# A transformer block's last product by Strassen's seven block products, 256 tokens at a time

## The chip, the cores and the metric

The kernel runs on one core of a Trainium2 chip, in one launch. Its engines are TensorE (PE; PEld is its weight load), VectorE (DVE), ScalarE (ACT), GpSimd (POOL) and SyncE (SP). SP issues all the DMAs here. The metric is the time of one execution in microseconds (us) on the device. A measurement of this kernel can tell a difference of about 0.3%.

## The reference, cut to what matters

Three layers follow each other: chunked attention, a SoLU layer with a layer norm, and a hard-swish layer. The change is in the hard-swish layer, the last one:

```python
def _moe2_ref(x, w_in, w_out):            # x: 3072 x 512, w_in: 512 x 2048, w_out: 2048 x 512
    h = x @ w_in
    relu6 = np.clip(h + 3.0, 0.0, 6.0)
    g = h * relu6 / 6.0
    return (g @ w_out).astype(np.float32)
```

The first product below is `x @ w_in`, the second is `g @ w_out`. The weights arrive as float64 words; the output is float32.

## The kernel before

To come close to float32 accuracy with operands of type float32r, each operand of a product is split into a high part (a copy into the type float32r, by ACT) and a low part (what remains, by DVE). The helper is `split`, lines 221 to 223. A product then takes three matmuls: high by high, high by low and low by high.

**Attention and SoLU stage** (to about 450 us). A step of the loop at line 707 does one tile of 128 tokens: both products of the SoLU layer and the attention of later tiles. Beside it the weights of the hard-swish layer are converted from float64 words (ACT, POOL, DVE) and stored to DRAM as float32 (`w2_store`, line 316). At the end of the last step come `split_x2(0)` and `split_w2(0)`, and behind them `ln_t` of the last tile and the twelve pieces of the last group's second SoLU product (`m2`).

**Hard-swish stage** (from about 450 us to the end). The tokens are taken in 8 groups of 384, the 2048 hidden columns in 16 blocks `f` of 128; a step is one pair (group, f), 128 steps in all.
- `g3` (line 619) makes one hidden block for the 384 tokens: 4 parts of the 512 inputs by 3 matmuls, so 12 matmuls with 384 moving columns. ACT takes the relu out of PSUM (line 628), DVE the min and product (line 629), and `split` makes the two parts `gh` and `gl`.
- `g4` (line 635), two steps later, adds this block's share to the output: for each of three tiles of 128 tokens, three matmuls with 512 moving columns, 9 in all. The three accumulators are scaled and stored at the end of a group (lines 649 to 654).

Each step's weights, high and low, are split in the first group and then stay in SBUF for all eight groups.

The program is in a fixed order: each engine runs its own instructions in the order in which the functions are called, and waits on semaphores where it needs another engine. SP is in order too, so a DMA that waits holds up the DMAs behind it.

## Time and profile before

| what | before |
|---|---|
| median of 3 runs | 989.15 us (988.51 to 990.86) |
| the profiled execution, span | 988.3 us |
| PE busy | 97% |
| DVE, ACT, POOL busy | 53%, 41%, 16% |
| chain that ended last | PE 89%, DVE 5%, DMA 3% |
| DMA | 86.72 MB, 88 GB/s over the span |

The times come from unprofiled runs, the rows from one profiled execution, whose span lies 0.85 us under the median. Matmuls are pipelined: a row's duration is the time that one takes from start to end, longer than the distance from one start to the next. How fast PE goes is read from the starts.

### The profile page before, as it was taken

What the parts mean: (1) busy time and instruction counts of PE and PEld (TensorE: products, weight loads), DVE (VectorE), ACT (ScalarE), POOL (GpSimd) and SP (SyncE); (2) the same over time, 40 slices, a digit from 0 to 9 for tenths busy, and PEclk for the clock granted to TensorE, in tenths of its full rate; (3) what the DMA queues carried; (4) which work ended last, traced back from release to release, by engine and by line L of the source; (5) the groups of instructions that cost most, each with busy time, mean ns of one, the idle gap of its engine ahead of it and who ended that gap; (6) DMA issues with size and microseconds to landing.
All of it is one profiled execution on the core that took longest, in us unless ns stands there. A gap on an engine that the chain in (4) does not pass through costs nothing.

```text
span 988.3 us, 15688 instructions
## 1 busy us (share of the span) xinstructions
PE 963.0 (97%) x6160; PEld 847.7 (86%) x6160; DVE 518.9 (53%) x921; ACT 408.5 (41%) x716; POOL 156.9 (16%) x123
## 2 busy tenths in 40 slices
PE   5899899999999999999999999999999999999998
PEld 4677788888888888899999999999999999999997
DVE  6999978787878776465532232232322322323222
ACT  2567635555564554344533232232332322323322
POOL 3637732423324240000000000000000000000000
PEclk9799999999999999999999999999999999999999
DMA  9897247656856672233401010010010010100000
GB/s 184 166 218 171 68 144 192 157 160 176 180 157 160 191 167 79 91 104 124 159 1 65 0 57 8 1 64 1 1 64 1 22 43 1 65 1 1 33 1 33
DMA packets 131769, 86.72 MB, mean 88 GB/s; under 512 B 105072, under 2 KB 117360, under 8 KB 131696
## 3 DMA queue, kind: packets, MB, share of 16 engines
q1 hardware_dynamic: 131696, 85.72, 33.4%
q8 instruction: 49, 0.80, 0.3%
q14 instruction: 24, 0.20, 0.1%
HBM read 64.72 MB, written 20.97 MB: 87 GB/s over the span
## 4 chain that ended last, share of the span: by engine, by line
PE 89%; DVE 5%; DMA 3%; issue 1%; SPq 1%; ACT 0%; POOL 0%; DVEq 0%; POOLq 0%
PE ph L625 27%; PE acc L646 27%; PE m L569 13%; PE h L484 11%; PE tp L453 2%; PE sc L397 2%; PE tp L541 2%; PE tp L371 2%; PE tp L372 1%; DMA km<-in_k_dram 1%; PE tp L384 1%; PE tp L435 1%; DMA mk<-in_mem_k_dram 1%; DMA w1raw<-in_moe_w_in_dram 0%; DMA w2d<-w2t 0%
## 5 line engine op out<-in xcount | busy, mean ns | idle before, releaser
L646 PE MATMUL acc<-w,gh 128*128 128x512 f32 x768 | 238.8, 392 | 0.0
L629 DVE SCALAR_TENSOR_TENSOR r<-r,ph 128x384 f32<-128x384 f32 x128 | 70.9, 554 | 278.3 <-ACT r L628 278.3
L628 ACT ACTIVATE r<-ph,three 128x384 f32<-128x384 f32 x128 | 74.4, 582 | 284.9 <-PE ph L625 284.9
L646 PEld LDWEIGHTS acc<-w,gh 128*128 128x128 f32 x768 | 142.3, 188 | 22.7
L646 PE MATMUL acc<-w,gl 128*128 128x512 f32 x384 | 151.1, 394 | 0.0
L625 PE MATMUL ph<-x,w 128*128 128x384 f32 x768 | 144.5, 336 | 0.0
L625 PE MATMUL ph<-x2h,w 128*128 128x384 f32 x512 | 141.0, 337 | 0.0
L625 PEld LDWEIGHTS ph<-x,w 128*128 128x128 f32 x768 | 136.0, 188 | 5.4
L223 DVE TENSOR_TENSOR gl<-r,gh 128x384 fp32r<-128x384 f32 x128 | 71.5, 559 | 75.7 <-ACT gh L222 75.7
L222 ACT ACTIVATE gh<-r 128x384 fp32r<-128x384 f32 x128 | 67.2, 525 | 80.1 <-DVE r L629 80.1
L625 PEld LDWEIGHTS ph<-x2h,w 128*128 128x128 f32 x512 | 93.7, 188 | 2.5
L569 PE MATMUL m<-lnh,wol 128*128 128x384 f32 x256 | 88.6, 346 | 0.9 <-POOL wol L313 0.9
L569 PE MATMUL m<-lnh,woh 128*128 128x384 f32 x256 | 88.4, 345 | 0.8 <-ACT woh L195 0.5
L569 PE MATMUL m<-lnl,woh 128*128 128x384 f32 x256 | 88.6, 346 | 0.3 <-DVE lnl L238 0.3
L625 PE MATMUL ph<-x2l,w 128*128 128x384 f32 x256 | 86.1, 336 | 0.0
L646 PEld LDWEIGHTS acc<-w,gl 128*128 128x128 f32 x384 | 72.0, 188 | 16.0
L484 PE MATMUL h<-w1h,xh 128*128 128x512 f32 x168 | 70.8, 421 | 0.0
L208 POOL TENSOR_SCALAR w2t<-w2t 128x512 f32<-128x512 f32 x32 | 64.9, 2040 | 28.2 <-ACT w2t L201 28.2
L484 PE MATMUL h<-w1h,xl 128*128 128x512 f32 x168 | 67.1, 400 | 1.7 <-DVE xl L238 1.7
L484 PE MATMUL h<-w1l,xh 128*128 128x512 f32 x168 | 66.6, 396 | 0.0
L234 ACT ACTIVATE lnh<-tp 128x512 fp32r<-128x512 f32 x41 | 24.3, 598 | 70.6 <-PE tp L541 70.5
L625 PEld LDWEIGHTS ph<-x2l,w 128*128 128x128 f32 x256 | 48.0, 188 | 2.5
(134 smaller groups left out, 1343.6 us busy)
## 6 DMA issues: line engine op xcount, KB each, us to landing
v<-in_v_dram SPq DMA_DIRECT2D x176, 56.0 KB
w2raw<-in_moe_w_in_dram SPq DMA_DIRECT2D x16, 512.0 KB
w2raw<-in_moe_w_out_dram SPq DMA_DIRECT2D x16, 512.0 KB
w2d<-w2t SPq DMA_DIRECT2D x32, 256.0 KB
...
```

What stands on the lines that cost most here:

```text
L208: ENG[eng].tensor_scalar(out=tf, in0=tf, scalar1=U_LO, scalar2=U_HI, op0=ALU.max, op1=ALU.min)
L222: ACT.activation(out=hi, in_=r, func=AF.Copy)
L223: (eng or DVE).tensor_tensor(lo, r, hi.bitcast(F32), ALU.subtract)
L234: ACT.activation(out=hi, in_=r, func=AF.Copy)
L371: PE.transpose(pt[:, j, 0:P], kn[i % 2][:, h:h + 2].rearrange("t h d -> t (h d)"), ident)
L397: PE.matmul(sc[64 * x:64 * x + 64, c, s], qb[:, p, c].rearrange("k y t -> k (y t)"), kT[:, p, c], start=True, stop=True)
L484: PE.matmul(h[:, f], a[:, kt], w[kt][:, f * 512:(f + 1) * 512], start=n == 0, stop=n == 3 * NKT - 1)
L569: PE.matmul(acc, w[fc // 2][:, fc % 2, dc * P:(dc + 1) * P], a[:, fc], start=n == 0, stop=n == len(todo) - 1)
L625: PE.matmul(ph, w[:, dc * P:(dc + 1) * P], xg[gi][a][:, dc], start=j == 0, stop=j == len(todo) - 1)
L628: ACT.activation(out=r, in_=ph, func=AF.Relu, bias=three, scale=1.0)
L629: DVE.scalar_tensor_tensor(out=r, in0=r, scalar=6.0, in1=ph, op0=ALU.min, op1=ALU.mult)
L646: PE.matmul(acc_t[t], a[:, sl], w, start=f == 0 and n == 0, stop=f == NF2 - 1 and n == 2)
```

## The change

A step now takes two hidden blocks (256 hidden columns) for a group of 256 tokens: 12 groups of 8 steps, 96 steps. `g3` makes both hidden blocks in one PSUM tile: 24 matmuls of 256 columns. The 2 x 2 blocks of `g` (two hidden blocks, two tiles of tokens) and the 2 x 2 blocks of the weights (two hidden blocks, two halves of the output columns) are multiplied by Strassen's method: seven products of sums and differences of blocks in place of eight, each with three matmuls of 256 columns, 21 in all. POOL makes the sums of `g` blocks (`act3`), ACT and DVE split them (`split3`), and the seven products are accumulated over a group in four PSUM banks and combined at its end by ACT, POOL and DVE (`g_out`, `g_end`).

The sums of weight blocks are made by POOL in the SoLU stage (`sum_pair`, stored to DRAM), read back and split (`prep`). A step's weights for the second product are 7 blocks of 128 x 256, high and low. They don't all fit: the steps 1, 4 and 7 of a group share one place in SBUF, so their split blocks are kept in DRAM and loaded again each time (`load_b`, seven DMAs). The attention and SoLU code keeps its order; some of its tiles get other places.

The diff, cut:

```diff
-    x2d = [dp.tile([P, NKT, G1], F32, name=f"x2d{i}") for i in range(NG)]
-    w2d = [dp.tile([P, 2, 512], F32, name=f"w2d{i}") for i in range(NF2)]
+    x2d = dp.tile([P, NKT, NT], F32, name="x2d")
+    w2d = [[dp.tile([P, 2, 512], F32, name=f"w2d{i}_{j}") for j in range(NF2 // 2)] for i in range(2)]
...
-        SP.dma_start(out=w2d[f][:, part], in_=raw["w2t", u].bitcast(F32))
+        SP.dma_start(out=w2d[part][f // 2][:, f % 2], in_=raw["w2t", u].bitcast(F32))
...
+    TG = 2 * P
+    NB = NT // TG
+    NS = NF2 // 2
+    USERS = (1, 4, 7)
+    B5_HOME = ("lh0", "lh1", "wb0", "wb1", "lh1", "ll1", "ll0", "lh1")
...
+    def load_pair(j):
+        raw["pair"] = T("xal", [P, 2, 2, 256], name="pair")
+        SP.dma_start(out=raw["pair"], in_=w2d[1][j].rearrange("p f (h c) -> p f h c", h=2))
+
+    def sum_pair(j):
+        w, t = raw["pair"], T("x2r", [P, 5, 256], name="sums")
+        POOL.tensor_tensor(t[:, 0:2], w[:, :, 0], w[:, :, 1], ALU.add)
+        POOL.tensor_tensor(t[:, 2], w[:, 0, 0], w[:, 1, 1], ALU.add)
+        POOL.tensor_tensor(t[:, 3], w[:, 0, 1], w[:, 1, 1], ALU.subtract)
+        POOL.tensor_tensor(t[:, 4], w[:, 1, 0], w[:, 0, 0], ALU.subtract)
+        SP.dma_start(out=b5f[j], in_=t)
...
+        for sl, t in parts:
+            split(t, b5[j][:, sl, 0], b5[j][:, sl, 1])
+        for k in range(2):
+            split(d[:, k], b2[j][k][:, 0], b2[j][k][:, 1])
...
+    def load_b(j):
+        for u in (2, 3, 4, 1, 0):
+            SP.dma_start(out=b5[j][:, u].bitcast(F32), in_=b5_d[j][:, u])
+        for n in (1, 0):
+            SP.dma_start(out=b2[j][n].bitcast(F32), in_=b2_d[j][:, n])
...
+    def g3(gi, j):
+        n = gi * NS + j
+        ph = pp.tile([P, 2, TG], F32, tag=("tp0", "tp1", "tp2", "sc")[n % 4], name="ph")
+        for k in range(2):
+            w = w2i[2 * j + k]
+            todo = [(dc, wl, xl) for dc in range(NKT) for wl, xl in ((0, 0), (0, 1), (1, 0))]
+            for m, (dc, wl, xl) in enumerate(todo):
+                PE.matmul(ph[:, k], w[:, wl, dc * P:(dc + 1) * P], xg[gi][xl][dc],
...
+    def act3(gi, j):
+        n = gi * NS + j
+        ph = ph_t.pop(n)
+        rt = home(("pn", "pe")[n % 2], 896, F32)
+        r = rt[:, 0:512]
         ACT.activation(out=r, in_=ph, func=AF.Relu, bias=three, scale=1.0)
         DVE.scalar_tensor_tensor(out=r, in0=r, scalar=6.0, in1=ph, op0=ALU.min, op1=ALU.mult)
-        gh = T(("kn0", "kn1", "q0")[n % 3], [P, 512], F32R, name="gh")[:, 0:G1]
-        gl = T(("km0", "km1", "q1")[n % 3], [P, 512], F32R, name="gl")[:, 0:G1]
-        split(r, gh, gl)
-        g_t[gi, f] = (gh, gl)
-
...
-    def g4(gi, f):
-                    acc_t[t] = late[0].tile([P, DM], F32, tag=f"m{t}", name="acc")
-                else:
-                    acc_t[t] = pp.tile([P, 2, DM], F32, tag="h", name="acc")[:, 0]
-            sl = slice(t * P, (t + 1) * P)
-            for n, (a, w) in enumerate(((gh, wh), (gh, wl), (gl, wh))):
-                PE.matmul(acc_t[t], a[:, sl], w, start=f == 0 and n == 0, stop=f == NF2 - 1 and n == 2)
-        if f == NF2 - 1:
-            for t in range(GT):
...
+    def split3(gi, j):
+        n = gi * NS + j
+        q = home(("pn", "pe")[n % 2], 896, F32).rearrange("p (b t) -> p b t", t=P)
+        s = home("xh", 512, F32).rearrange("p (b t) -> p b t", t=P)
+        tags = (("xah", "xal"), ("lh0", "ll0"))[n % 2]
+        ga = gA[n] = [extra(t)[:, 0:384].rearrange("p (b t) -> p b t", t=P) for t in tags]
+        split(q[:, 0:7:3], *ga)
+        tags = (("lh1", "ll1"), ("wb0", "wb1"))[n % 2]
+        gs = gS[n] = [extra(t).rearrange("p (b t) -> p b t", t=P) for t in tags]
+        split(s, *gs)
...
+    PRODUCTS = ((1, "A", 2, 5, 2), (3, "A", 0, 5, 3), (4, "A", 1, 5, 4), (5, "S", 0, 2, 1), (2, "S", 1, 2, 0),
+                (7, "S", 3, 5, 1), (6, "S", 2, 5, 0))
+    PLACE = {1: (0, 0), 3: (0, 1), 4: (1, 0), 5: (2, 0), 2: (2, 1), 7: (3, 0), 6: (3, 1)}
...
+    def g4(gi, j):
+        n = gi * NS + j
+        ga, gs = gA.pop(n), gS.pop(n)
+        for p, which, blk, wide, u in PRODUCTS:
+            a = ga if which == "A" else gs
+            w = b5[j][:, u] if wide == 5 else b2[j][u]
+            out = M(p)
+            for m, (al, wl) in enumerate(((0, 0), (0, 1), (1, 0))):
+                PE.matmul(out, a[al][:, blk], w[:, wl],
+                          start=j == 0 and m == 0 and PLACE[p][1] == 0, stop=j == NS - 1 and m == 2, skip_group_check=True)
...
+    def g_out(gi):
+        e = home("xl", 512, F32).rearrange("p (n c) -> p n c", n=2)
+        e1, e3, e4 = T("e5", [P, 1, 256], name="e1")[:, 0], e[:, 0], e[:, 1]
+        o1, o2 = T("xo0", [P, 512], name="o"), T("xo1", [P, 512], name="o")
+        o_t[:] = o1, o2, e3, e4
+        for t, n in ((e1, 1), (e3, 3), (e4, 4)):
+            ACT.activation(out=t, in_=M(n), func=AF.Copy, scale=1.0 / 6.0)
+        POOL.tensor_tensor(o1[:, 0:256], e1, e4, ALU.add)
+        POOL.tensor_tensor(o2[:, 256:512], e1, e3, ALU.add)
+
+    def g_end(gi):
+        o1, o2, e3, e4 = o_t
+        c11, c12, c21, c22 = o1[:, 0:256], o1[:, 256:512], o2[:, 0:256], o2[:, 256:512]
+        for o, n, sign, t in ((c12, 5, 1, e3), (c21, 2, 1, e4), (c11, 5, -1, c11), (c22, 2, -1, c22),
+                              (c11, 7, 1, c11), (c22, 6, 1, c22)):
+            DVE.scalar_tensor_tensor(out=o, in0=M(n), scalar=sign / 6.0, in1=t, op0=ALU.mult, op1=ALU.add)
+        for t, o in enumerate((o1, o2)):
+            SP.dma_start(out=out[gi * TG + t * P:gi * TG + (t + 1) * P, :], in_=o)
 
...
+            if m % 2:
+                if m < NTILE - 1:
+                    load_pair(m // 2 - 3)
+            elif m > STEADY:
+                sum_pair(m // 2 - 4)
+            if m == NTILE - 2:
                 load_x2(0)
-                load_w2f(0)
-                load_w2f(1)
+                load_prep()
+                load_prep()
             if m == NTILE - 1:
-                split_x2(0)
-                split_w2(0)
-                load_w2f(2)
+                split_x2(0, 0)
+                split_x2(0, 1)
+                load_wi(0)
+                prep()
+                prep()
+                split_wi(0)
+                load_wi(1)
         for j in range(4):
...
+            if j in (1, 6):
+                prep()
+            if j in (2, 5, 8):
+                w = (j + 1) // 3
+                split_wi(w)
+                load_wi(w + 1)
...
+        LAG = 2
+        for n in range(len(steps) + LAG):
             if n < len(steps):
-                gi, f = steps[n]
...
+                gi, j = steps[n]
+                g3(gi, j)
+                act3(gi, j)
+                if n + 4 < NS:
+                    split_wi(n + 4)
+                    if n + 6 < NS:
+                        load_wi(n + 6)
+                if n in (1, 2, 4, 7):
...
+                    store_prep()
+                if gi + 1 < NB:
+                    if j == 3:
                         load_x2(gi + 1)
-                    if f == 14:
-                        split_x2(gi + 1)
-            if n >= 2:
-                g4(*steps[n - 2])
+                    if j in (5, 6):
+                        split_x2(gi + 1, j - 5)
+            if n >= LAG:
+                gi, j = steps[n - LAG]
+                g4(gi, j)
+                if j in USERS and (gi > 0 or j == USERS[-1]):
+                    k = (USERS.index(j) + 1) % 3
+                    if not (gi == NB - 1 and k == 0):
+                        load_b(USERS[k])
+                if j == NS - 1:
+                    g_out(gi)
+            if n < len(steps):
+                split3(*steps[n])
+            if n >= LAG and j == NS - 1:
+                g_end(gi)
 
```

`USERS` are the steps that share a place; in `PRODUCTS` a row is the product's number, which set of `g` blocks it takes, the block in it, the width of the weight tile and the block there. `M(n)` is the accumulator of product n: products 1 and 3 share a bank, 5 and 2, 7 and 6; product 4 has one alone.

On PE, near the end of the program, one `g3` and the first two thirds of one `g4` stood like this (`ph` is the hidden block, `acc` an accumulator per tile of tokens, `gh` and `gl` the parts of `g`):

```order
L625 MATMUL ph_8863<-x2_8373,w2_5378 128x384 x12
L646 MATMUL acc_8503<-w2_5306,gh_8821 128x512 [waits Activation_49]
L646 MATMUL acc_8503<-w2_5307,gh_8821 128x512
L646 MATMUL acc_8503<-w2_5306,gl_8822 128x512 [waits DVE_49]
L646 MATMUL acc_8507<-w2_5306,gh_8821 128x512
L646 MATMUL acc_8507<-w2_5307,gh_8821 128x512
```

Now `g4` of a group's first step stands behind 24 matmuls of `g3`; here are the last matmul of `g3` and then the products 1, 3 and 4 (`acc_5272`, a tile of two banks), 5 and the beginning of 2 (`acc_5273`); `b_xah`, `b_xal`, `b_lh1`, `b_ll1` hold the parts of the `g` blocks and sums:

```order
L732 MATMUL ph_10087<-b_xah_4844,b_wa6_5022 128x256
L784 MATMUL acc_5272<-b_lh0_4959,b_xah_4844 128x256 [waits Activation_49]
L784 MATMUL acc_5272<-b_lh0_4959,b_xah_4844 128x256
L784 MATMUL acc_5272<-b_lh0_4959,b_xal_4845 128x256 [waits DVE_49]
L784 MATMUL acc_5272<-b_lh0_4959,b_xah_4844 128x256 x2
L784 MATMUL acc_5272<-b_lh0_4959,b_xal_4845 128x256
L784 MATMUL acc_5272<-b_lh0_4959,b_xah_4844 128x256 x2
L784 MATMUL acc_5272<-b_lh0_4959,b_xal_4845 128x256
L784 MATMUL acc_5273<-b_kn1_4961,b_lh1_5156 128x256 [waits DVE_49]
L784 MATMUL acc_5273<-b_kn1_4961,b_lh1_5156 128x256
L784 MATMUL acc_5273<-b_kn1_4961,b_ll1_5157 128x256
L784 MATMUL acc_5273<-b_kn0_4960,b_lh1_5156 128x256 x2
```

Nine matmuls of 512 columns became 21 of 256, and at a group's start product 1 waits for ACT and products 5 and 7 for DVE, which read these banks for the last group's result.

On SP, between two groups stood three stores of the output and one load of tokens:

```order
L654 DMA out_0_dram<-o_7991 128x512 [waits DMAHW7_49,Activation_49]
L654 DMA out_0_dram<-o_7994 128x512 [waits DMAHW0_49,DVE_49]
L654 DMA out_0_dram<-o_7997 128x512 [waits DMAHW1_49,Activation_49]
L605 DMA x2raw_8313<-x2d7_75 128x1536 [waits DMAHW6_49]
L654 DMA out_0_dram<-o_8474 128x512 [waits DMAHW3_49,Activation_49]
```

Now the seven loads of step 1's weights (`b5d1` and `b2d1` in DRAM to `b_lh1`, `b_km1`, `b_km0`) stand ahead of the stores:

```order
L706 DMA b_lh1_5156<-b5d1_94 128x512 [waits DMAHW1_49,PE_49]
L706 DMA b_lh1_5156<-b5d1_94 128x512 [waits DMAHW2_49,PE_49]
L706 DMA b_lh1_5156<-b5d1_94 128x512 [waits DMAHW3_49,PE_49]
L706 DMA b_lh1_5156<-b5d1_94 128x512 [waits DMAHW4_49,PE_49]
L706 DMA b_lh1_5156<-b5d1_94 128x512 [waits DMAHW5_49,PE_49]
L708 DMA b_km1_5202<-b2d1_97 128x512 [waits DMAHW6_49]
L708 DMA b_km0_5201<-b2d1_97 128x512 [waits DMAHW7_49]
L806 DMA out_0_dram<-o_10551 128x512 [waits DVE_49]
L806 DMA out_0_dram<-o_10552 128x512 [waits DMAHW0_49,DVE_49]
```

Each of the first five waits for PE, the reader of the block that it replaces.

On DVE, at the end of the last SoLU step, stood these between the last norm (`so`) and the low part of its transposed tile (`lnl`), for which PE waits:

```order
L534 TENSOR_SCALAR so_4745<-so_4745,lst_4713 128x1024
L223 TENSOR_TENSOR x2l_4770<-x2raw_4551,x2h_4769 128x768 x2
L223 TENSOR_TENSOR w2_4776<-w2f_4553,w2_4775 128x512 x2
L574 COPY x2o_4791<-m2_4748 128x384
L574 COPY x2o_4819<-m2_4794 128x384
L238 TENSOR_TENSOR lnl_4581<-tp_4822,lnh_4580 128x4x128
```

Now two calls of `prep` stand there too (`sums`, `b_x2r`, `b_t0`, `b_t1` are raw weight blocks, `w2i` raw weights of the first product):

```order
L542 TENSOR_SCALAR so_4820<-so_4820,lst_4788 128x1024
L223 TENSOR_TENSOR b_xal_4845<-x2raw_4742,b_xah_4844 128x512 x2
L223 TENSOR_TENSOR b_wb0_4853<-b_x2r_4744,b_wb0_4853 128x5x256
L223 TENSOR_TENSOR b_s0_4854<-b_t0_4745,b_s0_4854 128x256 x2
L223 TENSOR_TENSOR b_wb1_4864<-sums_4749,b_wb1_4864 128x4x256
L223 TENSOR_TENSOR b_wb1_4864<-sum_4750,b_wb1_4864 128x256
L223 TENSOR_TENSOR b_e1_4865<-b_t1_4751,b_e1_4865 128x256 x2
L223 TENSOR_TENSOR b_v0_4880<-w2i_4850,b_v0_4880 128x512
L223 TENSOR_TENSOR b_v1_4883<-w2i_4850,b_v1_4883 128x512
L582 COPY x2o_4897<-m2_4823 128x384
L582 COPY x2o_4925<-m2_4900 128x384
L238 TENSOR_TENSOR lnl_4636<-tp_4928,lnh_4635 128x4x128
```

The low part of the last tile now stands behind eleven subtractions in place of four.

## Rows read from the trace of the kernel before

**Rows 1.** The page's first part (busy time, share of the span, instructions) and its fourth (the chain that ended last, shares of the span by engine and by line).

```profile
PE 963.0 (97%) x6160; PEld 847.7 (86%) x6160; DVE 518.9 (53%) x921; ACT 408.5 (41%) x716; POOL 156.9 (16%) x123
...
PE 89%; DVE 5%; DMA 3%; issue 1%; SPq 1%; ACT 0%; POOL 0%; DVEq 0%; POOLq 0%
PE ph L625 27%; PE acc L646 27%; PE m L569 13%; PE h L484 11%; PE tp L453 2%; PE sc L397 2%; PE tp L541 2%; PE tp L371 2%; PE tp L372 1%; DMA km<-in_k_dram 1%; PE tp L384 1%; PE tp L435 1%; DMA mk<-in_mem_k_dram 1%; DMA w1raw<-in_moe_w_in_dram 0%; DMA w2d<-w2t 0%
```

**Rows 2.** Busy time by window, of the hard-swish stage: the stretch in us, its length, then busy us and instructions of each engine, the granted clock, the DMA share and GB/s.

```profile
450.00:984.00 534.00, 534.00 (x2690) 484.56 (x2688) 175.40 (x303) 171.59 (x309) 0.00 (x0) 1.00 0.09 32
```

**Rows 3.** Groups of PE's instructions by line and shape, with count, busy us, mean ns of one, and idle time before: the two products of the hard-swish layer, and the transposes.

```profile
L646 PE MATMUL acc<-w,gh 128*128 128x512 f32 x768 | 238.8, 392 | 0.0
L646 PE MATMUL acc<-w,gl 128*128 128x512 f32 x384 | 151.1, 394 | 0.0
L625 PE MATMUL ph<-x,w 128*128 128x384 f32 x768 | 144.5, 336 | 0.0
...
L625 PE MATMUL ph<-x2h,w 128*128 128x384 f32 x512 | 141.0, 337 | 0.0
...
L625 PE MATMUL ph<-x2l,w 128*128 128x384 f32 x256 | 86.1, 336 | 0.0
...
L541 PE MATMUL tp<-ident,so 128*128 128x128 f32 x192 | 28.9, 274 | 1.9 <-DVE so L534 1.7
```

**Rows 4.** The timeline of PE (start us, length us, what): the first and the last of the first 36 matmuls of the hard-swish stage, and the one behind them.

```profile
450.05 0.34 PE L625 MATMUL ph<-x2h,w 128*128 128x384 f32 x1
...
456.16 0.34 PE L625 MATMUL ph<-x2h,w 128*128 128x384 f32 x1
456.33 0.62 PE L646 MATMUL acc<-w,gh 128*128 128x512 f32 x2
```

**Rows 5.** The timeline of PE at the end: the first of the last 27 matmuls (the row holds two), and the last.

```profile
977.76 0.62 PE L646 MATMUL acc<-w,gh 128*128 128x512 f32 x2
...
983.73 0.39 PE L646 MATMUL acc<-w,gl 128*128 128x512 f32 x1
```

**Rows 6.** The timeline of PEld where products follow transposes, in the SoLU stage.

```profile
302.59 0.59 PEld L541 LDWEIGHTS tp<-ident,so 128*128 128x128 f32 x4
303.15 0.19 PEld L569 LDWEIGHTS m<-lnh,woh 128*128 128x128 f32 x1
303.26 0.19 PEld L569 LDWEIGHTS m<-lnl,woh 128*128 128x128 f32 x1
303.44 0.19 PEld L569 LDWEIGHTS m<-lnh,wol 128*128 128x128 f32 x1
```

**Rows 7.** Groups of DVE, ACT and POOL by line and shape (count, busy us, mean ns, idle time before).

```profile
L629 DVE SCALAR_TENSOR_TENSOR r<-r,ph 128x384 f32<-128x384 f32 x128 | 70.9, 554 | 278.3 <-ACT r L628 278.3
...
L427 POOL TENSOR_TENSOR pn<-pe,ast 128x512 f32<-128x512 f32 x20 | 21.9, 1096 | 26.7 <-DVE ast L423 14.2 <-ACT e L499 7.1 <-PE tp L541 5.4
...
L223 DVE TENSOR_TENSOR w<-w2f,w 128x512 fp32r<-128x512 f32 x32 | 20.6, 687 | 0.8 <-ACT w L222 0.8
L222 ACT ACTIVATE w<-w2f 128x512 fp32r<-128x512 f32 x32 | 18.2, 618 | 7.3 <-DMA w2f<-w2d 7.3
...
L653 ACT ACTIVATE o<-acc 128x512 f32<-128x512 f32 x16 | 8.7, 588 | 3.8 <-PE acc L646 3.8
...
L223 DVE TENSOR_TENSOR x2l<-x2raw,x2h 128x768 fp32r<-128x768 f32 x8 | 7.3, 955 | 0.5 <-ACT x2h L222 0.5
...
L222 ACT ACTIVATE x2h<-x2raw 128x768 fp32r<-128x768 f32 x8 | 6.3, 830 | 0.0
...
L313 POOL TENSOR_TENSOR wol<-wot,woh 128x512 fp32r<-128x512 f32 x2 | 3.4, 1678 | 0.1
```

**Rows 8.** Two timelines at the end of the SoLU stage: first DVE from the last norm to the last tile's low part, then PE from the last tile's transposes to the products behind them (in brackets the idle time before, and who ended it).

```profile
427.84 0.81 DVE L534 TENSOR_SCALAR so<-so,lst 128x1024 f32<-128x1024 f32 x1 [0.73 <-POOL lst L529]
428.57 1.82 DVE L223 TENSOR_TENSOR x2l<-x2raw,x2h 128x768 fp32r<-128x768 f32 x2
430.31 1.29 DVE L223 TENSOR_TENSOR w<-w2f,w 128x512 fp32r<-128x512 f32 x2
431.51 1.01 DVE L574 COPY x2o<-m 128x384 f32<-128x384 f32 x2
432.67 1.29 DVE L238 TENSOR_TENSOR lnl<-tp,lnh 128x512 fp32r<-128x512 f32 x2
...
431.40 1.03 PE L541 MATMUL tp<-ident,so 128*128 128x128 f32 x8
432.69 0.44 PE L569 MATMUL m<-lnh,woh 128*128 128x384 f32 x1 [0.25 <-ACT lnh L234]
433.42 0.45 PE L569 MATMUL m<-lnl,woh 128*128 128x384 f32 x1 [0.28 <-DVE lnl L238]
```

**Rows 9.** Windows (columns as in rows 2) around the one place after the start where the granted clock falls.

```profile
100.00:104.00 4.00, 2.16 (x14) 1.69 (x14) 3.84 (x11) 3.02 (x6) 1.67 (x2) 1.00 0.01 2
104.00:107.60 3.60, 3.60 (x12) 2.92 (x11) 3.60 (x5) 2.69 (x5) 3.17 (x3) 0.53 0.06 21
```

**Rows 10.** A window of the hard-swish stage while a group's tokens are loaded and the last group's output stored, and the page's GB/s in 40 slices of the span.

```profile
GB/s 184 166 218 171 68 144 192 157 160 176 180 157 160 191 167 79 91 104 124 159 1 65 0 57 8 1 64 1 1 64 1 22 43 1 65 1 1 33 1 33
...
523.00:527.00 4.00, 4.00 (x22) 3.61 (x21) 1.11 (x2) 1.11 (x2) 0.00 (x0) 1.00 0.91 319
```

**Rows 11.** The timeline of ACT at the very end: the last output tile taken out of PSUM.

```profile
984.15 0.60 ACT L653 ACTIVATE o<-acc 128x512 f32<-128x512 f32 x1 [0.76 <-PE acc L646]
```

More of the change, by code (lines that the diff above doesn't have):

```diff
@@ new lines, in sum_pair, with load_prep @@
+    def sum_pair(j):
[5 more added lines that the diff above has]
+        SP.dma_start(out=b5f[j], in_=t)
+    PREPS = (2, 3, 0, 6, 1, 5, 4, 7)
+    prep_n = [0, 0]
+    def load_prep():
+        n = prep_n[0]
+        prep_n[0] += 1
+        if n >= NS:
+            return
+        j = PREPS[n]
+        if n % 2 == 0:
+            t = home("x2r", 1536)[:, 0:1280].bitcast(F32).rearrange("p (u c) -> p u c", u=5)
+            parts = [(slice(0, 5), t)]
+        else:
+            parts = [(slice(0, 4), T("z1", [P, 4, 256], name="sums")), (slice(4, 5), T("e5", [P, 1, 256], name="sum"))]
+        d = home("xl", 512, F32) if n == NS - 1 else home(f"t{n % 2}", 512).bitcast(F32)
+        d = d.rearrange("p (k c) -> p k c", k=2)
+        for sl, t in parts:
+            SP.dma_start(out=t, in_=b5f[j][:, sl])
+        for k in range(2):
+            SP.dma_start(out=d[:, k], in_=w2d[1][j][:, k, 256 * k:256 * k + 256])
+        raw["prep", j] = parts, d
@@ L609, in split_x2 @@
+    def load_x2(gi):
+        raw["x2"] = T("z0", [P, NKT, TG], name="x2raw")
+        SP.dma_start(out=raw["x2"], in_=x2d[:, :, gi * TG:(gi + 1) * TG])
+    def split_x2(gi, n):
+        r = raw["x2"]
+        v3 = lambda t: t.rearrange("p (k t) -> p k t", t=TG)
         if gi % 2 == 0:
[L610 to L616 removed]
```

161 lines of the change are left out of this document (90 added, 71 removed).

## The prediction

> **What bounds the kernel now.** I read the page first: PE is busy 97% of the span, the chain that ended last is PE for 89%, and the two products of the hard-swish layer alone are 54% of it [rows 1]. The view by windows says the same of the stage that the change rewrites: from 450 to 984 us PE has no idle time, ACT and DVE are busy a third of it, POOL not at all, the DMAs 9%, and the granted clock is 1.00, the upper of its two levels, 2.4 GHz [rows 2]. So in this stage the time is the number of matmuls times the distance between their starts, and nothing else counts unless it makes PE wait.
>
> The durations of single matmuls, 336 and 392 ns [rows 3], overlap and are not that distance. The timeline gives it: 36 matmuls of 384 columns start from 450.05 to 456.16, which is 6.11 us for 35 distances, 174.6 ns each [rows 4]. The last 27 of 512 columns start from 977.76 to 983.73: 5.97 us for 26, 229.6 ns each [rows 5]. The stage starts at 450.05 and its last matmul would hand over 0.23 us after 983.73, so it is 533.9 us long. 768 + 512 + 256 = 1536 matmuls [rows 3] at 174.6 are 268.2 us; the other 265.7 us over 768 + 384 = 1152 are 230.6 each. I keep 229.6 to 230.6.
>
> **The change on PE.** The first product: 96 steps of 24 matmuls, 2304 of 256 columns: as many columns as 1536 of 384. The second: 96 x 21 = 2016 of 256 columns, against 1152 of 512: an eighth fewer columns. In all 4320 matmuls in place of 2688, each with its own weight load. No matmul of 256 columns with such operands is in the trace, so its distance decides. The straight line through 384 and 512 gives 174.6 - 55.0 to 174.6 - 56.0: 118.6 to 119.6 ns. I take 119.1, so 4320 x 0.1191 = 514.5 us, 19.4 less than 533.9.
>
> Both ends for that distance: a matmul can't go faster than its columns at 2.4 GHz, 106.7 ns, nor than its weight load. PEld's rows show two loads for products 303.15 and 303.26, 110 ns apart, where the first matmul didn't hold up the second load; the next comes 180 later, behind a matmul [rows 6]. Eight transposes of 128 columns take 1.03 us [rows 8] with 274 ns for the last one [rows 3], so 7 distances of 108: there the load sets the pace. From above, the recorded load lasts 190 ns [rows 6], and if loads couldn't overlap, 190 would be the distance; but 174.6 is already less than that. So from 110 to 190, and I am near the lower end because the line is.
>
> **Around it.** (a) A step is 45 x 0.1191 = 5.36 us. DVE does in it 512, 384 and 512 columns: 0.69, 0.55 and 0.69 us; ACT about 0.6 + 0.5 + 0.6 [rows 7]; POOL three sums of 640 columns in all, an operation that it has done at 1.10 to 1.68 us per 512 [rows 7], so 1.4 to 2.1 us. All are far below 5.36. From the end of `g3` to the last low part the chain is 0.6 + 0.7 + (1.4 to 2.1) + 0.6 + 0.7, at most 4.7 us, and `g4` needs it two steps later, after 10.7 us. Cost 0; the 6 us to spare also hide the four `prep` calls of the first group (DVE about 2.3 us each).
>
> (b) The end of the SoLU stage. DVE ended its last norm at 428.65 and then did 2 x 0.95 + 2 x 0.69 us of splits before the copies and the last low part, for which PE waited until 433.42 [rows 7, 8]. Now it has 2 x 0.69, and two `prep` of 1280 + 2 x 256 columns (the second in one part more), and 2 x 0.69. At 1.04 us per 1000 columns and 0.15 us per instruction (from 687 and 955 ns for 512 and 768 columns) that is 1.4 + 2.3 + 2.5 + 1.4 = 7.6 us against 3.3. Then the copies (1.0) and the low part (0.7): 428.6 + 9.3 = 437.9 against 433.4: PE waits 4.4 us more. In such a gap the clock may fall: where PE was busy 2.16 of 4 us, the granted clock was 0.53 in the next 3.6 us, about the lower level, 1.2 GHz [rows 9]. That stretch at half speed costs 1.7 us. Together +6.1. Bounds: 3 (some of the splits lie where DVE waited for ACT anyway, and the clock stays) to 10 (the loads for `prep` land late as well).
>
> (c) Group changes. After the last product of a group at T, PE has 24 matmuls of `g3` and the products 1, 3 and 4 to do, so it wants to start product 5 at T + 3.9 and product 7 at T + 4.6 us. DVE must first have read those banks. It starts its six combinations (0.42 us each by (b)'s figures) only behind that step's splits: relu from T - 2.5, then 0.6 + 0.7, POOL 1.4 to 2.1, ACT 0.6, DVE 0.7, which is T + 1.5 to 2.2; four combinations are done at T + 3.2 to 3.9, six at T + 4.0 to 4.7. A wait of 0 to 0.6 us with the handovers; I take 0.2, 11 times: +2.2.
>
> GpSimd's rows differ by half for the same operation [rows 7]. The Trainium skill (GPSIMD Engine Reference, Key points) says that GpSimd shares its SBUF interfaces with VectorE and contends with DVE instructions that read two SBUF operands. The low parts of `split3` are such; by that rule the slow end, 2.1 us, holds, and (c) would be 0.3 to 0.6 each, 3 to 7 in all; no row here says which operation stood beside which.
>
> (d) The reload. A load is 7 x 128 rows of 2 KB, 1.835 MB, three per group. The shortest time for it is from step 7 to step 1 of the next group: the blocks come free one by one in the last 2.1 us before T, the next user's `g4` starts after 24 + 21 + 24 matmuls, T + 8.2, and its last-loaded block is wanted 12 matmuls later, T + 9.7. With transfers beginning about T - 1.1 and 1 us of latency that leaves 9.8 us: 187 GB/s are enough. In this stage the chip moved 319 GB/s over 4 us [rows 10], which is 5.8 us. Cost 0.
>
> (e) The end. The last tile left PSUM at 984.75 [rows 11] and the span ended 3.5 us later. Now six combinations of 0.42 stand between the last product and the store, so about 6.0 us in place of 4.2 after the last matmul: +1.8. (f) `sum_pair` puts 8 x 1280 columns on POOL, some 30 us in a stage in which it is busy 157 of 450 [rows 1], and eight more loads and stores on SP: 0, at most 2.
>
> Sum: 988.3 - 533.9 + 514.5 + 6.1 + 2.2 + 1.8 = 979.0, by the profiled execution. The median of the runs lies 0.85 above that execution's span, so I forecast 980. The gain of 19.4 less 10.1 of new costs: at a distance of 121.3 ns nothing is left.
>
> **Rivals.**
> 1. The columns alone count, or the load: 112 ns, where the 14 ns over the columns' time at 384 were a matter of long matmuls. For it: load to load 108 to 110. Against: 174.6 and 230 are 14.6 and 16.7 over their columns' time, so that most of it stays. 4320 x 0.112 = 483.8, 949 us. The Trainium skill (TensorE: Matmul & The Clock Gate, Back-to-back issue gap) gives columns / 2.4 + 2.5 ns, so 109.2 ns here, an estimate of 937 us; by that rule 384 columns take 162.5, and the trace, 174.6, does not agree.
> 2. Slower: at 256 columns the load (108 to 110) is as long as the stream (107), and what comes over it is added to the longer one of them, with the two in each other's way: 108 + 15 to 17, about 124 ns, in every matmul of the stage. 535.7 us, 1001 in all. It decides from 122 ns on, where the sum is over 0.3% slower. For it: no row has the two so close; against: at 384 the load is 62% of the distance and nothing shows of it.
> 3. The reload comes late, if the many 2 KB rows go only at the 160 to 190 GB/s of the slices of the SoLU stage [rows 10]: 1.835 MB take 10.9 us, late by 1.1, 11 times: 992 us. Against: 319 GB/s.
> 4. The group change costs 1 us rather than 0.2 (POOL at 2.9 us): 989.
>
> **Chances and range.** The forecast 0.50 (its own range 973 to 988: 117.5 to 121 ns), rival 1 0.09, rival 2 0.19, rival 3 0.10, rival 4 0.12. What a measurement can tell is 0.3%, 3 us. Faster: 0.46 of the forecast, all of rival 1, 0.05 of rival 4: 0.60. Same: 0.04, 0.03 of rival 2, 0.05 of rival 3 and 0.05 of rival 4: 0.17. Slower: 0.16 + 0.05 + 0.02 = 0.23. Range 957 to 1003: it leaves out rival 1's own figure, and of rivals 2 and 3 what would lie over 1003.
>
> **What would show it.** In the new profile: 24 matmuls of `g3` and 21 of `g4` at 119 ns from start to start; PE busy over 98% of the last stage, with gaps only at group changes, of 0.2 us, ended by DVE; one gap of 4 to 5 us ahead of the last SoLU group's products, ended by DVE's low part, with a clock below 1 behind it; no PE wait for a DMA of `load_b`; some 60 MB more read. A distance over 121 ns, or waits for DMA at step 1, would make it wrong.

## The result and the profile after

The changed kernel takes 1005.48 us (median of four runs, 1002.72 to 1006.63), the kernel before 990.0 beside it: ratio 1.0149, 95% interval 1.0129 to 1.0169. It is 1.5% slower; 980 us were forecast. The profiled execution took 1006.11 us, with a span of 1004.3 against 988.3.

The page of the changed kernel, the parts of [rows 1]:

```profile
PE 953.8 (95%) x7792; PEld 882.9 (88%) x7792; DVE 606.0 (60%) x1037; ACT 453.9 (45%) x788; POOL 433.1 (43%) x467
...
HBM read 132.62 MB, written 31.72 MB: 164 GB/s over the span
...
PE 61%; DVE 12%; POOL 11%; issue 11%; DMA 2%; ACT 2%; SPq 0%; POOLq 0%; DVEq 0%; ACTq 0%
```

PE is busy for 9 us less than before, but the chain that ended last is PE for only 61% of the span, where it was 89%. DVE and POOL together have 23%: wherever PE waits for them, the chain goes back through their work. That is not PE's idle time; the waits below are some 26 us in all. Who ended them, before 420 us and behind it (us in total, times, longest):

```profile
PE tp L443 <- POOL pn L435: 9.9, 7, 1.9
...
PE acc L784 <- DVE o L804: 10.7, 11, 3.4
PE m L577 <- DVE x2o L582: 3.4, 1, 3.4
PE acc L784 <- DVE b_xal L223: 0.8, 1, 0.8
PE acc L784 <- DVE b_ll L223: 0.8, 1, 0.8
```

Here `pn` is the softmax's result and `tp` its transpose, `m` the second SoLU product in PSUM and `x2o` its copy out of it, `b_xal` and `b_ll` low parts of `g` blocks and of their sums. Before, the row of the transposes for `pn` on POOL was 1.8 us in one wait, ahead of the tenth tile; that one has stayed, and the six new ones are 8.1 us. The product's own waits are for `o`, the combinations at the eleven group changes. No row names a DMA of `load_b`.

The windows of the hard-swish stage, which answer to [rows 2]:

```profile
490.00:520.00 30.00, 29.82 (x251) 29.82 (x252) 19.91 (x31) 15.58 (x29) 15.28 (x18) 1.00 0.60 228
520.00:535.00 15.00, 11.63 (x76) 11.43 (x75) 7.02 (x14) 4.66 (x10) 5.77 (x8) 0.77 0.54 188
535.00:600.00 65.00, 64.29 (x542) 64.08 (x542) 28.16 (x47) 25.17 (x43) 29.44 (x38) 1.00 0.47 152
600.00:800.00 200.00, 196.30 (x1650) 195.30 (x1650) 87.77 (x149) 76.47 (x133) 91.81 (x121) 1.00 0.46 153
```

From 600 to 800 us PE is busy for 196.30 us with 1650 matmuls: 119.0 ns each, where 119.1 were forecast. It is idle for 3.7 us, five group changes. Busy time also counts the tail of the last matmul ahead of a wait, 0.16 us at each change; from start to start, where nothing waits and the clock is full, the matmuls of the stage are 118.4 ns apart. From 520 to 535 PE does only 76 matmuls at a clock of 0.77: that is the first group change.

Where the time went, by the starts of matmuls in PE's timelines (tenth and last SoLU tile, first and last matmul of the hard-swish stage):

| stretch | before, us | after, us | difference | forecast |
|---|---|---|---|---|
| start to the tenth SoLU tile | 176.3 | 177.8 | +1.5 | 0 |
| tenth to last SoLU tile | 237.6 | 249.8 | +12.3 | 0 (f) |
| last SoLU tile to hard-swish | 36.2 | 41.2 | +5.0 | +6.1 (b) |
| hard-swish, first to last matmul | 533.7 | 529.7 | -4.0 | -19.4 + 2.2 (c) |
| behind the last matmul starts | 4.6 | 5.9 | +1.3 | +1.8 (e) |

The first row isn't explained, nor much in need of it: in the runs below, whose code is the same there up to the SoLU steps, that stretch took 175.1 to 177.5.

### Where the SoLU steps lose

Before, every step took 17.2 us. After, only every second one does. The timeline of POOL in such a step, first before, then after (start, length, what):

```profile
212.24 1.92 POOL L208 TENSOR_SCALAR w2t<-w2t 128x512 f32<-128x512 f32 x1
214.60 1.04 POOL L427 TENSOR_TENSOR pn<-pe,ast 128x512 f32<-128x512 f32 x1 [0.44 <-DVE ast L423]
```

```profile
213.73 3.97 POOL L208 TENSOR_SCALAR w2t<-w2t 128x512 f32<-128x512 f32 x2 [2.01 <-ACT w2t L201]
217.66 1.46 POOL L647 TENSOR_TENSOR sums<-pair 128x512 f32<-128x512 f32 x1
219.07 1.19 POOL L648 TENSOR_TENSOR sums<-pair 128x256 f32<-128x256 f32 x1
220.22 1.18 POOL L649 TENSOR_TENSOR sums<-pair 128x256 f32<-128x256 f32 x1
221.37 0.71 POOL L650 TENSOR_TENSOR sums<-pair 128x256 f32<-128x256 f32 x1
222.05 1.04 POOL L435 TENSOR_TENSOR pn<-pe,ast 128x512 f32<-128x512 f32 x1
...
223.14 0.66 PE L443 MATMUL tp<-ident,pn 128*128 128x128 f32 x4 [1.79 <-POOL pn L435]
```

The four sums of `sum_pair`, 4.4 us, stand ahead of the next tile's `pn`, because the loop issues them at the end of a step and `s_norm` at the start of the next. PE's transposes of `pn` wait 1.79 us. POOL is idle for 7 us behind that. Six such waits are 8.1 of the 12.3 us; most of the rest is the clock, which fell behind one of them (last section).

### Where the group change loses

DVE and PE at the second group change (the last product of the group hands over at 568.15), then POOL beside it:

```profile
568.43 0.56 DVE L223 TENSOR_TENSOR b_ll<-b_pe,b_lh 128x384 fp32r<-128x384 f32 x1 [1.13 <-ACT b_lh L222]
570.28 1.26 DVE L223 TENSOR_TENSOR b_wb<-b_xh,b_wb 128x512 fp32r<-128x512 f32 x1 [1.29 <-ACT b_wb L222]
571.46 0.74 DVE L804 SCALAR_TENSOR_TENSOR o<-acc,b_xl 128x256 f32<-128x256 f32 x2
572.13 1.40 DVE L804 SCALAR_TENSOR_TENSOR o<-acc,o 128x256 f32<-128x256 f32 x4
...
571.93 0.28 PE L784 MATMUL acc<-b_lh,b_xal 128*128 128x256 f32 x1
572.92 0.50 PE L784 MATMUL acc<-b_kn,b_lh 128*128 128x256 f32 x2 [0.71 <-DVE o L804]
...
568.50 1.09 POOL L749 TENSOR_TENSOR b_xh<-b_pe 128x256 f32<-128x256 f32 x1
569.55 0.74 POOL L796 TENSOR_TENSOR o<-e,b_xl 128x256 f32<-128x256 f32 x1
570.25 0.74 POOL L797 TENSOR_TENSOR o<-e,b_xl 128x256 f32<-128x256 f32 x1
```

The low part of the step's sums (`b_wb`) takes DVE 1.26 us; its usual length is 0.69. POOL's last addition runs from 570.25 to 570.99, and 570.99 + 0.55 is the end of the low part: it stood still until POOL was done. Earlier, POOL's third sum (L749) had met DVE's low part of the single blocks (`b_ll`, to 568.99) in the same way: 1.09 us, where it takes 0.73 with nothing of that kind beside it (last section). Only then come the combinations; the fourth ends at 572.8 (572.13 and half of 1.40) and product 5 starts 0.99 us behind the matmul before it, 0.87 late. Its second matmul comes 0.1 us late as well, so that such a change costs 1.0 us.

### The profile page after: what moved, and what is told of

It reads as the page before. It is cut to its first block, busy times and chain, and to the rows that moved or that the text cites. A ratio compares the mean times of both kernels' runs of the same rounds, so it can differ in the third digit from the quotient of the medians.

```text
span 1004.3 us, 20271 instructions
## 1 busy us (share of the span) xinstructions
PE 953.8 (95%) x7792; PEld 882.9 (88%) x7792; DVE 606.0 (60%) x1037; ACT 453.9 (45%) x788; POOL 433.1 (43%) x467
## 4 chain that ended last, share of the span: by engine, by line
PE 61%; DVE 12%; POOL 11%; issue 11%; DMA 2%; ACT 2%; SPq 0%; POOLq 0%; DVEq 0%; ACTq 0%
PE ph L732 20%; PE acc L784 17%; PE m L577 10%; PE h L492 7%; POOL b_xh L749 3%; PE tp L461 2%; POOL b_xh L748 2%; DMA q_raw<-in_q_dram 2%; DVE o L804 2%; DVE b_wb L223 2%; PE sc L405 1%; PE tp L379 1%; POOL w2t L208 1%; POOL pn L435 1%; PE tp L380 1%
## 5 line engine op out<-in xcount | busy, mean ns | idle before, releaser
L492 PE MATMUL h<-w,xh 128*128 128x512 f32 x336 | 110.5, 410 | 0.0
L732 PE MATMUL ph<-b_x2r,b_wa 128*128 128x256 f32 x480 | 92.2, 283 | 0.0
L732 PE MATMUL ph<-b_xah,b_wa 128*128 128x256 f32 x480 | 90.7, 280 | 0.0
L732 PEld LDWEIGHTS ph<-b_x2r,b_wa 128*128 128x128 f32 x480 | 77.1, 191 | 0.0
L732 PEld LDWEIGHTS ph<-b_xah,b_wa 128*128 128x128 f32 x480 | 76.1, 189 | 0.0
L223 DVE TENSOR_TENSOR b_wb<-b_xh,b_wb 128x512 fp32r<-128x512 f32 x48 | 39.4, 820 | 59.5 <-ACT b_wb L222 59.5
L492 PEld LDWEIGHTS h<-w,xh 128*128 128x128 f32 x336 | 61.0, 192 | 11.7
L492 PE MATMUL h<-w,xl 128*128 128x512 f32 x168 | 67.1, 399 | 1.9 <-DVE xl L238 1.9
L732 PE MATMUL ph<-b_t,b_wa 128*128 128x256 f32 x240 | 67.7, 282 | 0.0
L732 PE MATMUL ph<-b_xal,b_wa 128*128 128x256 f32 x240 | 67.4, 281 | 0.0
```

Source lines behind the costliest of these rows:

```text
L223: (eng or DVE).tensor_tensor(lo, r, hi.bitcast(F32), ALU.subtract)
L492: PE.matmul(h[:, f], a[:, kt], w[kt][:, f * 512:(f + 1) * 512], start=n == 0, stop=n == 3 * NKT - 1)
L732: PE.matmul(ph[:, k], w[:, wl, dc * P:(dc + 1) * P], xg[gi][xl][dc], start=m == 0, stop=m == len(todo) - 1)
```

## The experiments

All times are medians with the kernel before run on the same chip; gains are against 1005.5 us.

### The sums behind the softmax's multiplication

```diff
 ...
 s_norm(a, "P")
+if m % 2 and STEADY < m < NTILE - 1:
+    sum_pair((m - 1) // 2 - 4)
...
-elif m > STEADY:
+elif m == NTILE - 2:
     sum_pair(m // 2 - 4)
```

> Theory A (GpSimd's order): the 12.3 us that the SoLU steps lost between their starts at 177.8 and 379.4 us come from the four additions and subtractions of the weight blocks (4.5 us) that stand ahead of the softmax's multiplication in GpSimd's row; with them right behind that multiplication the six waits of the transposes for pn (0.8 to 1.9 us) and the half clock after the longest go, every step is 17.2 us from the next, and the time is 1005.5 - 12.3 = 993 us (990 to 998). Rival B (transfers): the eight added loads and eight stores on SyncE's queue hold the loads of the queries back; they are all still there, so the steps stay long and the time stays at 1003 to 1008 us.

997.63 us (ratio 1.0072, 1.0057 to 1.0087): 8 of 12.3. The six waits for `pn` are gone, the SoLU steps take 241.9 us, and a new wait has come, six times (`pb` is ACT's copy of the transposed softmax):

```profile
PE tp L461 <- ACT pb L195: 4.0, 6, 1.0
```

POOL and DVE in the same step of this run:

```profile
215.79 1.21 POOL L435 TENSOR_TENSOR pn<-pe,ast 128x512 f32<-128x512 f32 x1
216.96 1.73 POOL L647 TENSOR_TENSOR sums<-pair 128x512 f32<-128x512 f32 x1
218.66 1.19 POOL L648 TENSOR_TENSOR sums<-pair 128x256 f32<-128x256 f32 x1
...
216.14 1.41 DVE L215 SCALAR_TENSOR_TENSOR w2t<-w2raw,w2t 128x512 uint32<-128x512 uint32 x1
217.58 1.66 DVE L218 SCALAR_TENSOR_TENSOR w2t<-w2raw,w2t 128x512 uint32<-128x512 uint32 x1
219.17 0.68 DVE L238 TENSOR_TENSOR lnl<-tp,lnh 128x512 fp32r<-128x512 f32 x1
```

L215 and L218 take 0.69 us with POOL idle. Here L218 ends 0.55 us behind POOL's first sum (216.96 + 1.73 = 218.69, and 219.24): it stood still for that sum. The second sum, 1.19 us where the last of its size took 0.71 above, was shut out in its turn by L218. L238, which takes one of its inputs from PSUM, is not slowed by the second sum beside it. DVE's lateness passes through the SoLU layer's maximum, which ends at 220.98, and the exponential, which ACT starts at 221.01, to `pb` behind it on ACT, for which PE waits.

The Trainium skill (SBUF — State Buffer, Who interferes with whom) states this: a DVE instruction with two SBUF inputs contends with a GpSimd instruction that reads SBUF, over a port pair that is an exclusive lock, and a DVE instruction with at most one SBUF input, outside the 2-port modes, does not. The ends of L218 and L238 here, and of the low part at 571.54 above, agree.

### The sums left out, and the sums in two steps

```diff
-w, t = raw["pair"], T("x2r", [P, 5, 256], name="sums")
-POOL.tensor_tensor(t[:, 0:2], w[:, :, 0], w[:, :, 1], ALU.add)
...
-SP.dma_start(out=b5f[j], in_=t)
+w = raw["pair"].rearrange("p a b c -> p (a b) c")
+SP.dma_start(out=b5f[j][:, 0:4], in_=w)
+SP.dma_start(out=b5f[j][:, 4:5], in_=w[:, 0:1])
```

> GpSimd's additions of the weight blocks are left out; what was loaded is stored instead, so that the loads and stores on SyncE's queue stay (one store more for each pair) and only GpSimd's 4.5 us every second step go. Theory A (GpSimd): the SoLU steps take 237.6 us from the start of the tenth to that of the last again, as before, instead of 249.8, no transpose waits for pn after the tenth step, and the time is 993 us (991 to 996). Rival B (transfers): the steps take over 245 us and the time is 1001 us or more.

993.08 us (1.0024, 1.0015 to 1.0033) and 238.4 us for the steps. All loads and stores are still there, so transfers aren't the cause: POOL's work in this place is, for 12.4 us of the time.

Next, the first sum behind `s_norm` in even steps, the other three and the store in odd ones (`sum_pair` takes the half as its second argument; this is its call):

```diff
 ...
 s_norm(a, "P")
+if STEADY < m < NTILE - 2:
+    sum_pair((m - 8) // 2, m % 2)
 ...
```

> The four additions stand behind the softmax's multiplication, as in e1_sums_later, but the first (1.5 us) in one step and the other three (2.6 us) in the next. Theory C: in e1_sums_later the weight conversion on VectorE ran beside all 4.3 us of GpSimd and lost 1.7 us, which reached TensorE as six waits for pb of 0.6 to 1 us; with half of it in a step VectorE loses under 1 us, which the step's slack takes: steps 237.6 to 239 us, time 1005.5 - 11 = 994 (992 to 996). Rival: every loss of VectorE there reaches TensorE, twelve waits of half the length: steps near 242 us, time 997 us as in e1_sums_later.

992.93 us (1.0025, 1.0015 to 1.0034). All the sums are computed, and 12.5 us are back, as many as without the sums. In the profiled execution, the slowest of the ten (995.23), PE waits for `pb` four times, 2.2 us, and the steps take 240.3 us, 1.9 more than without the sums; the medians don't show that.

### The combinations ahead of the split

```diff
+if n >= LAG and j == NS - 1:
+    g_end(gi)
 if n < len(steps):
     split3(*steps[n])
-if n >= LAG and j == NS - 1:
-    g_end(gi)
```

> Theory A: the wait at each group change (0.9 us at ten of them, 3.4 at the first) is VectorE's order, the six combinations standing behind the low part of the step's split; with them ahead of it they end 1.3 to 2 us earlier, product 5 waits under 0.3 us at ten changes and 2 to 2.5 at the first: 1005.5 - 9 - 1 = 995 us (993 to 998). Rival B: the third and fourth combination need GpSimd's two sums, which stand behind GpSimd's three operations of the step; VectorE waits there, holds the step's split behind it, and the wait of TensorE only moves: 1003 to 1006 us.

987.36 us (0.9974, 0.9957 to 0.9992): 18.1 us less, from swapping two calls. The hard-swish stage falls from 529.7 to 515.2 us. PE's waits in it:

```profile
PE acc L784 <- DVE o L804: 1.6, 1, 1.6
PE acc L784 <- DVE b_xal L223: 0.8, 1, 0.8
PE acc L784 <- DVE b_ll L223: 0.5, 1, 0.5
```

Ten of the eleven waits for `o` are gone. The expectation was too small mainly because it left out the clock: behind the first group change's 3.4 us the changed kernel ran at a clock of 0.50 from 525.8 to 532.6, which cost 2.8 us; behind the wait of 1.6 us here the clock stayed at 1.00. The rest of the 18 us, some 3.5, is in stretches that the edit doesn't touch and that vary from run to run.

The next edit keeps the two calls swapped and lets the first four combinations do without POOL's additions, which come last instead:

```diff
 ...
-POOL.tensor_tensor(o1[:, 0:256], e1, e4, ALU.add)
-POOL.tensor_tensor(o2[:, 256:512], e1, e3, ALU.add)
...
-(c11, 5, -1, c11), (c22, 2, -1, c22)
+(c11, 5, -1, e4), (c22, 2, -1, e3)
...
+for o in (c11, c22):
+    POOL.tensor_tensor(o, o, e1, ALU.add)
```

> As e2_end_first, and the first four combinations no longer read GpSimd's two sums: they take ScalarE's copies, and GpSimd adds the third copy to the two finished pieces at the end. Theory: the 1.6 us that are left at the first group change in e2_end_first are the wait for those two sums, which stand behind GpSimd's 2.3 us of the step; they go, and the time is 987.4 - 1.6 = 986 us (984.5 to 987). Rival: what is left there is VectorE's own lag of 2.6 us behind TensorE after the first group's weight preparations; the wait stays over 1 us, and the additions at the very end (0.7 us before the last output) lengthen the tail: 987 to 989 us.

987.25 us (0.9978, 0.9959 to 0.9997). The last wait for `o` is gone and the stage takes 513.5 us, 1.6 less, as the theory says; in the medians the two versions can't be told apart.

### The reload

```diff
-if not (gi == NB - 1 and k == 0):
+if gi == 0 and k:
     load_b(USERS[k])
```

> The reloads of the three weight blocks are left out from the second group on (later groups multiply by what lies in the buffer). If the reload costs nothing, as forecast, the time is that of the changed kernel, 1005.5 us within 1.5. Rival: the 20 MB more of reading slow the matmuls' operands or the engines' access to the same memory, and the time falls by 5 us or more, with distances below 118 ns.

1002.12 us, 3.4 less, outside the 1.5 that were allowed. The reads from HBM fell from 132.6 to 72.1 MB, by 60.6 rather than the expectation's 20. But the stage in which the reloads lay went from 529.7 to 528.6 us only, with the same distances. From 600 to 800 us, where the DMAs now idle:

```profile
600.00:800.00 200.00, 196.28 (x1649) 195.28 (x1648) 87.86 (x148) 76.46 (x133) 91.87 (x121) 1.00 0.08 28
```

PE is busy 196.28 us with 1649 matmuls, before it was 196.30 with 1650, at 28 GB/s in place of 153. The reload costs nothing there; the other 3 to 4 us are in the SoLU steps, 246.1 against 249.8 us with the same code: their clock stayed at 1.00 in this run (last section).

### The weight preparations at the end of the SoLU stage

DVE there in the changed kernel, and the two PE rows that wait:

```profile
442.34 1.28 DVE L223 TENSOR_TENSOR b_xal<-x2raw,b_xah 128x512 fp32r<-128x512 f32 x2
443.55 1.48 DVE L223 TENSOR_TENSOR b_wb<-b_x2r,b_wb 128x1280 fp32r<-128x1280 f32 x1
...
447.76 1.29 DVE L223 TENSOR_TENSOR b_v<-w2i,b_v 128x512 fp32r<-128x512 f32 x2
448.96 1.02 DVE L582 COPY x2o<-m 128x384 f32<-128x384 f32 x2
...
449.66 0.41 PE L577 MATMUL m<-lnh,woh 128*128 128x384 f32 x1 [3.45 <-DVE x2o L582]
450.63 0.65 PE L577 MATMUL m<-lnl,woh 128*128 128x384 f32 x1 [0.56 <-DVE lnl L238]
```

Four edits tried to take these 3.5 us away, and none gained beyond the scatter of its runs. The first:

```diff
 ...
 load_wi(0)
-prep()
-prep()
-split_wi(0)
-load_wi(1)
...
 ln_t(NTILE - 1, 1)
+prep()
+prep()
+split_wi(0)
+load_wi(1)
```

> Two of the eight weight preparations and one split are moved behind the last tile's splits. Theory A: TensorE's wait of 3.5 + 0.6 us at 446 us, and the 3 us at half clock after it, come from VectorE's 7.6 us of splits ahead of the copy that frees the accumulator; without 6 us of them the wait is under 1 us and the time 1005.5 - 5 = 1000.5 us (999 to 1002). Rival B: VectorE has no room for them in the 18 us behind either, so TensorE waits there for the same time: 1004 to 1007 us.

1006.45 us (1.0146, 1.0108 to 1.0184). In the trace, of the fastest of its four runs (999.14; the others took 1005.8 to 1007.5), the wait at this place fell to 0.25 + 0.28 us, but PE waits 2.0 us for a later copy and 1.8 us in the first group.

```diff
-prep()
-prep()
+prep(POOL)
+prep(POOL)
```

> The low parts of the two weight preparations at the end of the SoLU stage are computed on GpSimd instead of VectorE (GpSimd is idle there from 442 to 468 us). Theory: TensorE's wait for x2o falls from 3.5 to under 1 us and the half clock behind it goes: the stretch from the last SoLU step to the first hard-swish product falls from 41.2 to 37 us, time 1005.5 - 4 = 1001.5 (1000 to 1003). Rival: GpSimd's long subtractions slow VectorE's two-input operations beside them (as in e1_sums_later, where 0.69 us became 1.4 to 1.7), and the stretch falls by less than 2 us: 1003.5 to 1006.

1004.27 us (1.0143, 1.0114 to 1.0172): the rival, and more. The stretch grew to 44.3 us, and PE's wait to 5.5. Two splits that take 1.29 us alone took 3.96, shut out by POOL's subtractions beside them. Ahead of them DVE stood idle for 3.54 us, until ACT had split the same weights, whose load had come late; so even without the 2.7 us of exclusion PE would have waited some 2.8 us, an estimate from these rows, and the theory's under 1 us was out of reach:

```profile
442.68 3.96 DVE L223 TENSOR_TENSOR b_v<-w2i,b_v 128x512 fp32r<-128x512 f32 x2 [3.54 <-ACT b_v L222]
...
441.93 1.41 POOL L223 TENSOR_TENSOR b_s<-b_t,b_s 128x256 fp32r<-128x256 f32 x2
443.29 2.79 POOL L223 TENSOR_TENSOR b_wb<-sums,b_wb 128x1024 fp32r<-128x1024 f32 x1
```

The third had the later preparations behind the copies too:

```diff
-if j in (1, 6):
-    prep()
 if j in (2, 5, 8):
     ...
+if j in (2, 8):
+    prep()
 ...
```

> As e3_preps_later, and the third and fourth preparation stand behind the copies that free the accumulators instead of ahead of them. Theory: e3_preps_later gained nothing because its wait of 3.5 us only moved, to 2.0 us for the next copy, held up behind a preparation that waited for its load; with the copies first no wait over 1 us is left in the stretch, which falls from 41.2 to 37 us: 1005.5 - 4 = 1001.5 us (1000 to 1003). Rival: VectorE, 20 us of work in 23 us, is late into the first group instead, and the gain comes back there as waits for the splits: 1003.5 to 1007 us.

1007.19 us (1.0172, 1.015 to 1.0194); the stretch took 43.4 us. The same edit with the two others:

> All three: e10_two_fixes and e11_preps_behind_copy together. 974.8 - 4 = 971 us (969 to 974), ratio 0.980; if e11's rival holds, 974 to 976.

982.57 us (0.9924, 0.9912 to 0.9937), against 977.8 without it (below). Its DVE shows why:

```profile
440.04 0.55 DVE L582 COPY x2o<-m 128x384 f32<-128x384 f32 x1
446.24 0.69 DVE L223 TENSOR_TENSOR b_qb<-w2i,b_qb 128x512 fp32r<-128x512 f32 x1 [5.65 <-ACT b_qb L222]
```

DVE stands still for 5.65 us ahead of a split whose weights are not loaded yet, and the next copies stand behind it. The first five loads of `load_wi` share one buffer, so that the next load starts only when a split has emptied it; the edit had put DVE's first split 4.6 us later (10.7 us behind the last norm in place of 6.1). The last edit laid the splits where their loads have landed:

```diff
 ...
 ln_t(NTILE - 1, 1)
+prep()
+split_wi(0)
+load_wi(1)
 for j in range(12):
     ...
+    if j in (2, 5, 8):
+        prep()
+    if j in (5, 8, 11):
+        w = (j - 2) // 3
         split_wi(w)
         load_wi(w + 1)
```

> As e10_two_fixes, with one preparation and the first split of the first product's weights behind the last tile's splits, the other preparations each behind the next copy that frees an accumulator, and the splits of the first product's weights one place later. Theory: e11_preps_behind_copy and e12_three_fixes gained nothing because the one buffer into which those weights are loaded makes a chain (load 5 us, split, next load), their first split came 6 us later, and the copies stood behind a split that waited for its load (5.7 us); with the splits placed where their loads have landed no wait over 1 us is left in the stretch from the last SoLU step to the hard-swish stage, which falls from 41.7 to 37 us: 977.8 - 4.5 = 973.5 us (971.5 to 975.5), ratio 0.983. Rival: VectorE's 20 us of work in these 23 us can't be laid out without a wait of some microseconds somewhere; the stretch stays over 40 us and the time at 976.5 us or more.

978.65 us (0.9874, 0.9852 to 0.9897), where 973.5 were expected. The stretch takes 36.2 us, as before the change: the theory on the order was right there. But the chain of loads now ends too late for the first group:

```profile
PE acc L788 <- ACT b_xah L222: 4.2, 1, 4.2
```

ACT's split of the first step stands behind splits that wait for their loads. The 4 us only moved. Whether a second load buffer would free them wasn't tried.

### Both fixes

> The edits of e9_sums_halved and e5_end_no_pool together. They stand in different stages, so their gains should add: 1005.5 - 12.5 - 18.2 = 974.8 us (973 to 977), ratio to the kernel before 0.984. Rival: a part of each gain is the same clock level lost and won (the clock falls after a wait of TensorE, and each run wins it back at another place), and the sum is not reached: 977 to 981 us.

977.82 us (0.9875, 0.9862 to 0.9889): the two edits that gained, together, make a kernel faster than both; it is 1.2% faster than the one before. The sum of the single gains, 974.8, is not reached, and the time lies 0.8 us inside the rival's range; the runs, 976.6 to 979.5, don't decide between the two. One row of its trace shows the stage nearly free of waits, 118.5 ns of busy time for each matmul:

```profile
456.00:968.00 512.00, 510.66 (x4310) 510.25 (x4310) 248.88 (x398) 209.24 (x368) 241.11 (x310) 1.00 0.49 161
```

## Why the prediction was wrong

**The distance: right, and 0.7 ns too long.** 119.1 ns were taken from the line through 384 and 512 columns; 118.4 were measured from start to start. 4319 distances are 511.4 us, 22.3 less than the stage's 533.7. Rivals 1 and 2 fall: neither the bare columns nor a weight load that adds to them. By the formula of the Trainium skill (TensorE: Matmul & The Clock Gate, Back-to-back issue gap), columns / 2.4 + 2.5 ns, it would be 109.2 ns, an estimate; the trace doesn't agree, by 9 ns here and by 12 at 384 columns.

**(f) failed: 0, at most 2, was 12.4 us.** The step counted POOL's busy time (157 of 450 us) and overlooked its order. The 30 us fit into POOL's idle time, but not there: they stood in a queue ahead of an operation on which PE waits in the same step. Of the 12.3 us in the profiled execution 8.1 are those waits and some 3.5 the half clock behind one of them. The sums left out brought all of it back, and moved by one place and halved, they cost no more than left out (992.9 against 993.1). The transfers on SP, the other half of that step, cost nothing either. None of the rivals had this mechanism.

**(c) failed in size: 0.2 x 11 = 2.2 us was taken; from start to start the ten later changes cost 1.0 us each, the first one 3.5, and the clock behind it 2.8, together 16.3.** The runs bear it out: without these waits the stage takes 513.5 instead of 529.7 us. The mechanism, the combinations behind the split, was the right one. At the second change, with the group's end at 568.15, the low part was to end 1.5 to 2.2 us behind it and ended 3.4 behind: POOL's three sums took from 567.38 to 569.59, 2.2 us against at most 2.1, with the third shut out for 0.35; the relu came 0.25 us later than taken; and the low part itself took 1.26 us rather than 0.7, shut out by POOL's two additions for the output. The fourth combination was to end by 3.9 and ended at 4.7. Rival 4 had the size, about 1 us, but put it on POOL's sums at 2.9 us, which they were not. The contention that the forecast cited from the Trainium skill (GPSIMD Engine Reference, Key points) is there, with about 0.57 us on DVE at each change, though no edit took it away by itself; the price set on it, 3 to 7 us in all, had left out that POOL's own output additions lie beside the low part. The two rows that the forecast read as one operation, 1.10 and 1.68 us, also differ in their operands: `pn` multiplies by one value per row of the softmax and takes 1.04 us at its shortest, an operation on two full inputs of 512 columns 1.27.

**(a) was wrong for the first group.** The 6 us of slack didn't hide the four preparations: at the first change DVE's step behind the relu starts 1.13 us behind the group's end, at the second 1.53 ahead of it, so that DVE is 2.7 us late. That the preparations made it late is read from the trace, where the last of them ends at 515.1; no run tests it. The first change waited 3.4 us instead of some 0.7, the clock was 0.50 behind it, and two waits of 0.8 us, 2.1 from start to start, came in the steps before. With (c) these make the stage: 511.4 + 16.3 + 2.1 = 529.8, where 529.7 were measured. With the combinations ahead of the split and free of POOL, the same late DVE cost nothing at the change.

**(b) right:** +6.1 forecast, +5.0 measured, with the wait, its place and the clock behind it as described (0.50 from 450.7 to 454.1), though the longer wait was for the copy, 3.45 us, and only 0.56 for the low part. **(d) right:** no wait for the reload, no slower matmul beside it, with 67.9 MB more read (some 60 were forecast); rival 3 falls. The 1 us that was taken there for a transfer's latency stands in no row, and nothing came to hang on it. **(e) right** within half a us.

With (f) and (c) taken out, the change is worth what the distance promised less (b), (e) and some remains: 977.8 us. That this is near the forecast of 980 is no merit of the forecast: its kernel had both faults in it.
